# Attention and soft mixture of experts on one core: the second expert layer cut into units of 128, 256 and 128 columns

## The chip, the cores and the metric

The kernel runs on one core of a Trainium2 chip. The metric is the device time of one execution in microseconds (us). Everything is fp32.

## The reference

Two steps follow each other. The first is an attention between 512 tokens `x` and 32 states in each of 8 batches and 8 heads; its output, tokens and states together, is a matrix `x` of 8 * 544 rows and 512 columns. The second is a soft mixture of 8 experts with 4 slots each:

```python
logits = x @ phi                                  # 4352 x 32
d = softmax over the rows (axis 0) of logits
slot_input = d.T @ x                              # 32 slots x 512
for e in range(8):
    h = np.maximum(slot_input[e] @ w1[e], 0.0)    # 4 x 1024
    slot_out[e] = h @ w2[e]                       # 4 x 512
c = softmax over the slots (axis 1) of logits
return c @ slot_out                               # 4352 x 512
```

The weights `w1` (8 x 512 x 1024) and `w2` (8 x 1024 x 512) are 16 MB each, so a core must read some 32 MB of weights and 8 MB of `x` and write some 9 MB of output.

## The kernel before, in words

The program has three stages. The attention is written as a table of steps (`ORDER`, lines 30 to 56) that is walked at line 679; it ends with the 32 slot inputs. Then comes the first expert layer: `w1_part` (line 695) adds up `h_ps` for the two halves `hf` of the 1024 hidden columns, `h_copy` brings a half to SBUF, `h_turn` (line 714) transposes it, and `h_relu` (line 719) sums and clips it into `h_m[hf]`. Then comes the second layer with the output.

The change is in the last stage. The 512 columns of `w2` are handled in **units**: a unit has a PSUM tile `so[k]` in which the products of all 8 experts and both hidden halves are added up (16 parts of 4 matmuls of 32 rows, `part` at line 756). Before, unit 0 has columns 0 to 255, unit 2 columns 256 to 383 and unit 3 columns 384 to 511. When a unit is complete,

- `so_copy` (line 774) copies it to SBUF (ACT takes the first 128 columns, DVE the next 128),
- `so_sum` (line 782) adds its four row groups by a matmul with `rep`, for 128 columns at a time, and ACT copies the result into `so_r`,
- `out(k, q)` (line 790) multiplies block `k` of 128 output columns with the token weights of four batches `q` (4 matmuls of 512 columns), ACT and DVE copy two of the four results each into a tile `out`, and SyncE (SP) stores it by one DMA of 1024 KB; `out(0, 0)` alone is stored in two halves. `out_st` does the same for the states, `out_by_batches` for block (3, 0), in two halves.

The order of PE's work is written out by hand at lines 874 to 914: between the `out` blocks stand calls `more(n)`, which issue the next `n` parts of the units that are still to come. Every DMA of weights and of outputs is issued by SP, in the order of the program, so that all go through one queue. `load_w` (line 108) issues the weights from the list `todo`, one at a time, whenever a buffer of the attention has become free; `load_part` (line 136) puts three experts of `w2` into small buffers (`st_phi`, four `h` tiles, `sv`). The last weights, two tiles `w2b` of 2048 KB, are issued during the first layer at line 707.

Of the kernel before, what the change touches and what calls it, by code (L numbers as in the profile page):

```python
# [8 lines left out]
F32 = mybir.dt.float32  # L9
# [6 lines left out]
P = 128  # L16
B = 8
S = 512
NS = 32
D = 64  # L20
E = 8
F = 1024
# [34 lines left out]
SR_BUFS = 1  # L57
AN = 2

GROUPS = ((0, 1), (2, 3), (4, 5), (6, 7))  # L60


@with_exitstack
def attention_soft_moe(ctx: ExitStack, tc: tile.TileContext, x0, x1, x, st0, st1, w1, w2a, w2b, out_x, out_s):

# [3 lines left out]
    nc = tc.nc  # L71
    pe, act, dve, pool = nc.tensor, nc.scalar, nc.vector, nc.gpsimd
# [4 lines left out]
    pairs = ctx.enter_context(tc.tile_pool(name="pairs", bufs=NPAIR))  # L77


    st_phi = cp.tile([P, F + 4 * NS], F32, name="st_phi")  # L80
# [3 lines left out]
    for b in range(B):  # L84
        t = big.tile([P, 4, NJ, 2 * D], F32, tag="big", name=f"x{b}")
# [14 lines left out]

    w1t, w2t = {}, {}
    todo = [(1, hf, e) for hf in range(2) for e in range(E)]
    todo += [(2, k, e) for k in range(2) for e in range(0, E, 2)]
    last = todo.pop()
    todo += [(3, 0, 0), (3, 0, 4), last, (3, 1, 0), (3, 1, 4)]
    both = []

    def load_w(n):
        for _ in range(min(n, len(todo))):
            layer, k, e = todo.pop(0)  # L110
            if layer == 3:
                t = pairs.tile([P, 4 * F], F32, tag="pair", name=f"w3_{k}_{e}")
                t = t.rearrange("p (e k f) -> p e k f", e=4, k=8)
                nc.sync.dma_start(t, w2b[e // 4, k])
                for i in range(32):
                    w2t[3, k, e + i // 8, i % 8] = t[:, i // 8, i % 8]
                continue
            if layer == 1 and len(w1t) < 8 * NPAIR:
                if not both:
                    t = pairs.tile([P, 4 * F], F32, tag="pair", name=f"w1_{k}_{e}")  # L120
                    both.extend((t[:, 0 : 2 * F], t[:, 2 * F :]))
                t = both.pop(0)
            else:
                t = big.tile([P, 2 * F], F32, tag="big", name=f"w{layer}_{k}_{e}")
            if layer == 1:
                t = t.rearrange("p (k f) -> p k f", k=4)
                nc.sync.dma_start(t, w1[k, e])
                for i in range(4):
                    w1t[k, e, i] = t[:, i]
            else:  # L130
                t = t.rearrange("p (e k f) -> p e k f", e=2, k=4)
                nc.sync.dma_start(t, w2a[e // 2, k])
                for i in range(8):
                    w2t[layer, k, e + i // 4, i % 4] = t[:, i // 4, i % 4]

    def load_part(t, k, e, ft):
        n = t.shape[1] // 256
        t = t.rearrange("p (k f) -> p k f", k=n)
        nc.sync.dma_start(t, w2a[e // 2, k][:, e % 2, ft : ft + n])
        for i in range(n):  # L140
            w2t[2, k, e, ft + i] = t[:, i]

    def st_t(b, g):
        return stT_sb[:, b // 2, g % 2, g // 2, b % 2, :]
# [29 lines left out]
    with ExitStack() as actx:  # L174
        wk = actx.enter_context(tc.tile_pool(name="work", bufs=1))
# [14 lines left out]
        def half(name):  # L190
            return wk.tile([P, S], F32, tag="h", name=name, bufs=NH)
# [483 lines left out]

        states_read = max(order.index(f"S.{B - 1}"), order.index("U.1"))
        halves_had = max(order.index(t) for t in order if t.split(".")[0] in ("q", "aT", "e2", "ee", "ed", "windows"))
        (k1, e1), (k2, e2) = [todo.pop(B)[1:] for _ in range(2)]
        for i, step in enumerate(order):
            name, *args = step.split(".")  # L680
            steps[name](*map(int, args))
            if i == states_read:
                load_part(st_phi[:, 0:F], k1, e1, 0)
            if i == halves_had:
                for k, e in ((k1, e1 + 1), (k2, e2)):
                    for ft in (0, 2):
                        load_part(half(f"w2_{k}_{e}_{ft}"), k, e, ft)
        load_part(wk.tile([P, 2 * S], F32, tag="sv", name=f"w2_{k2}_{e2 + 1}", bufs=1), k2, e2 + 1, 0)


        h_ps = [ps_s.tile([P, 512], F32, tag="sc", name=f"h_ps{i}") for i in range(2)]
# [22 lines left out]
        def h_turn(hf):  # L714
            hT[hf] = ps_t.tile([P, 4, P], F32, tag="tr", name=f"hT_ps{hf}")
            for ft in range(4):
                pe.transpose(hT[hf][:, ft, :], h_sb[hf][:, P * ft : P * ft + P], ident)

        def h_relu(hf):
            t = sm.tile([P, 4, NS], F32, tag="tt", name=f"hT{hf}", bufs=1)  # L720
            dve.tensor_reduce(out=t, in_=hT[hf].rearrange("p f (k n) -> p f n k", k=4), axis=AX.X, op=ALU.add)
            for ft in range(4):
                dve.tensor_scalar_max(slots(h_m[hf], ft), t[:, ft, :].rearrange("p (e c) -> p e c", c=4), 0.0)
# [28 lines left out]


        so, so_sb, so_r = {}, {}, {}

        def part(k, hf, e, cols, w):
            if hf == 0 and e == 0:
                so[k] = ps_s.tile([P, cols], F32, tag="sc", name=f"so_ps{k}")
            for i in range(4):
                pe.matmul(  # L760
                    so[k][32 * i : 32 * i + 32, :],
                    h_m[hf][:, 256 * i + 32 * e : 256 * i + 32 * e + 32],
                    w(i),
                    start=(hf == 0 and e == 0),
                    stop=(hf == 1 and e == E - 1),
                )

        def wide_part(hf, e):
            part(0, hf, e, 256, lambda i: w2t[2, hf, e, i])

        def w2_part(k, hf, e):
            part(k, hf, e, P, lambda i: w2t[3, k - 2, e, 4 * hf + i])

        def so_copy(k):
            cols = so[k].shape[1]
            so_sb[k] = half(f"so_sb{k}")[:, 0:cols]
            act.copy(so_sb[k][:, 0:P], so[k][:, 0:P])
            if cols > P:
                dve.tensor_copy(so_sb[k][:, P:cols], so[k][:, P:cols])

        def so_sum(k, half_of=0):
            c = slice(P * half_of, P * half_of + P)
            p = mtile([P, P], f"sum_ps{k}_{half_of}")
            pe.matmul(p, rep, so_sb[k][:, c], start=True, stop=True)
            i = k + half_of
            if i % 2 == 0:
                so_r[i // 2] = half(f"so_r{i // 2}")[:, 0:256]
            act.copy(so_r[i // 2][:, P * (i % 2) : P * (i % 2) + P], p)

        def out(k, q):  # L790
            hf, col = k // 2, 128 * (k % 2)
            o = [(ps_t if j % 2 else ps_m).tile([P, 512], F32, tag="tr" if j % 2 else "ms", name=f"o{k}_{q}_{j}")
                 for j in range(NJ)]
            for j in range(NJ):
                rows = slice(32 * j, 32 * j + 32)
                pe.matmul(  # L796
                    o[j],
                    so_r[hf][rows, col : col + 128],
                    lt_all[rows, 4 * q : 4 * q + 4, :].rearrange("p b s -> p (b s)"),
                    start=True,  # L800
                    stop=True,
                )
            ot = big.tile([P, NJ, 512], F32, tag="big", name=f"out{k}_{q}")
            to = out_x[k, q].rearrange("p j s -> (p j s)").rearrange("(i p j s) -> i p j s", i=2, p=P, j=2)
            for jp in range(2):
                act.copy(ot[:, 2 * jp, :], o[2 * jp])  # L806
                dve.tensor_copy(ot[:, 2 * jp + 1, :], o[2 * jp + 1])  # L807
                if (k, q) == (0, 0):
                    nc.sync.dma_start(to[jp], ot[:, 2 * jp : 2 * jp + 2, :])
            if (k, q) != (0, 0):  # L810
                nc.sync.dma_start(out_x[k, q], ot)

        def out_by_batches(k, q):
            hf, col = k // 2, 128 * (k % 2)
# [56 lines left out]
                        c_back(i)  # L871
            h_copy(hf)

        for e in range(E):
            wide_part(0, e)
            if e == 3:
                h_turn(1)
                h_relu(1)
        for e in range(E):
            wide_part(1, e)  # L880

        rest = [(k, hf, e) for k in (2, 3) for hf in range(2) for e in range(E)]

        def more(n):
            for _ in range(n):
                w2_part(*rest.pop(0))

        so_copy(0)
        more(1)
        so_sum(0)  # L890
        more(1)
        so_sum(0, 1)
        out(0, 0)
        more(5)
        out(0, 1)
        more(5)
        out(1, 0)
        more(4)
        so_copy(2)
        out(1, 1)  # L900
        so_sum(2)
        more(4)
        out_st(0)
        out_st(1)
        out(2, 0)
        more(6)
        out(2, 1)
        more(6)
        so_copy(3)
        out_st(2)  # L910
        so_sum(3)
        out_by_batches(3, 0)
        out_st(3)
        out(3, 1)
# [35 lines left out]
```

## Time and profile before

| what | value |
|---|---|
| median of 3 runs | 129.48 us (129.45 to 129.86) |
| the profiled execution | 129.54 us, of which its span is 127.8 us |
| PE busy | 116.7 us, 91% of the span |
| DVE, ACT, POOL busy | 68%, 60%, 35% |
| DMA | 51.74 MB, mean 405 GB/s |
| DMA busy share | full (9 of 9) in all of the 40 slices but the first and the last |

A busy share of the DMA is the mean over 16 DMA engines. "To landing" is the time from the start of a DMA's issue on SP until the last of its engines has reported its part. The chain of waits is the work that ended last, followed back from the end; a line of it gives the start, the length and the work.

### The profile page before, as it was taken

The page shows a single profiled execution, that of the slowest core. Times are in us where ns is not written, and L with a number is a line of the kernel's source. Part 1 is how long each engine was busy: PE and PEld are TensorE (multiplying, and loading weights), DVE is VectorE, ACT ScalarE, POOL GpSimd, SP SyncE. Part 2 cuts the span into 40 slices and gives each one's busy share as a digit, 9 for nine tenths or more (in the row PEclk, how much of TensorE's full clock was granted, in tenths as well). Part 3 has the DMA queues.
Part 4 walks back from the last instruction along what each step waited for, and adds up shares of the span by engine and source line. Part 5 has one row for each costly group of instructions (what it writes and reads, how often), then busy time and mean ns, then how long its engine had stood idle before and what let it go on. Part 6 is the DMA issues. An engine that isn't in the chain of part 4 may idle for free.

```text
span 127.8 us, 4698 instructions
## 1 busy us (share of the span) xinstructions
PE 116.7 (91%) x1992; PEld 80.5 (63%) x1992; DVE 86.7 (68%) x194; ACT 76.9 (60%) x189; POOL 44.8 (35%) x63
## 2 busy tenths in 40 slices
PE   5989999999999999999999999999999999998600
PEld 2737686789686869858767869952465655575200
DVE  2348999999999999999986759019930355442700
ACT  4039999999999999999965711310100445635700
POOL 3005266391947467557882105803500000000000
PEclk9999999999999999999999999999999999999955
DMA  4999999999999999999999999999999999999993
GB/s 130 345 410 423 423 426 423 428 423 421 423 423 426 416 436 416 421 431 418 426 418 433 416 421 398 448 423 441 413 441 415 436 383 412 421 419 420 386 430 139
DMA packets 8229, 51.74 MB, mean 405 GB/s; under 512 B 912, under 2 KB 1040, under 8 KB 3216
## 3 DMA queue, kind: packets, MB, share of 16 engines
q1 hardware_dynamic: 7920, 50.92, 95.9%
q10 hardware_dynamic: 288, 0.52, 1.1%
q8 instruction: 15, 0.25, 0.7%
q14 instruction: 6, 0.05, 0.1%
HBM read 42.53 MB, written 8.91 MB: 403 GB/s over the span
## 4 chain that ended last, share of the span: by engine, by line
PE 72%; DVE 10%; DMA 6%; ACT 3%; issue 2%; SPq 1%; POOL 0%; DVEq 0%; ACTq 0%; POOLq 0%
PE so_ps L760 12%; PE h_ps L697 11%; PE xt_ps L226 8%; PE o L796 7%; DMA st_phi<-st_in 6%; PE sc L245 5%; PE sr_ps L343 4%; PE an_ps L309 4%; PE eT_ps L309 4%; PE lt L378 3%; PE t_ps L503 2%; DVE sums L274 2%; DVE q L258 2%; DVE aT L290 1%; DVE m L263 1%
## 5 line engine op out<-in xcount | busy, mean ns | idle before, releaser
L267 POOL TENSOR_TENSOR q<-q,m 128x512 f32<-128x512 f32 x16 | 16.8, 1051 | 15.7 <-DVE m L263 5.2
L231 ACT ACTIVATE xt<-xt_ps 128x512 f32<-128x512 f32 x30 | 18.0, 618 | 5.7 <-PE xt_ps L226 5.5
L226 PE MATMUL xt_ps<-ident,x 128*128 128x128 f32 x128 | 18.4, 282 | 0.5 <-DMA x<-x_in 0.5
L285 POOL TENSOR_TENSOR q<-q,rr 128x512 f32<-128x512 f32 x16 | 16.6, 1051 | 5.1 <-DVE rr L280 3.6
L226 PEld LDWEIGHTS xt_ps<-ident,x 128*128 128x128 f32 x128 | 14.6, 144 | 3.8 <-PE sc L245 1.4
L760 PE MATMUL so_ps<-w,h_m 128*32 128x128 f32 (+1 forms) x376 | 15.5, 309 | 0.0
L807 DVE COPY out<-o 128x512 f32<-128x512 f32 x14 | 9.2, 687 | 9.0 <-PE o L796 8.8
L760 PEld LDWEIGHTS so_ps<-w,h_m 128*32 128x32 f32 x376 | 10.4, 110 | 7.2 <-issue 4.6
L697 PE MATMUL h_ps<-w,si_m 128*32 128x512 f32 x128 | 14.4, 594 | 0.1
L296 DVE TENSOR_REDUCE nm<-sc 128x1 f32<-128x512 f32 x16 | 10.6, 670 | 2.2 <-PE sc L245 2.2
L806 ACT COPY out<-o 128x512 f32<-128x512 f32 x14 | 7.7, 588 | 6.8 <-PE o L796 6.7
L697 PEld LDWEIGHTS h_ps<-w,si_m 128*32 128x32 f32 x128 | 9.1, 110 | 3.9 <-issue 2.9
L301 ACT ACTIVATE e<-sc,nm 128x512 f32<-128x512 f32 x16 | 11.3, 709 | 0.4 <-DVE nm L296 0.2
L258 DVE STREAM_TRANSPOSE q<-sc 128x512 f32<-128x512 f32 x16 | 11.1, 695 | 0.1
L290 DVE STREAM_TRANSPOSE aT<-q 128x512 f32<-128x512 f32 x16 | 10.9, 689 | 0.3 <-POOL q L285 0.2
L343 PE MATMUL sr_ps<-x,eT 128*32 128x64 f32 x512 | 10.5, 221 | 0.1
L274 DVE TENSOR_REDUCE sums<-q 128x16 f32<-128x512 f32 x16 | 10.4, 663 | 0.2 <-ACT q L270 0.2
L263 DVE TENSOR_REDUCE m<-q 128x16 f32<-128x512 f32 x16 | 10.4, 658 | 0.0
L270 ACT ACTIVATE q<-q 128x512 f32<-128x512 f32 x16 | 10.4, 650 | 0.0
L309 PE MATMUL eT_ps<-ident,e 128*128 128x128 f32 x64 | 9.8, 279 | 0.0
L245 PE MATMUL sc<-xt,st_phi 64*32 64x512 f32 x128 | 9.6, 601 | 0.0
L343 PEld LDWEIGHTS sr_ps<-x,eT 128*32 128x32 f32 x512 | 8.7, 110 | 1.5 <-issue 1.0
(126 smaller groups left out, 186.2 us busy)
## 6 DMA issues: line engine op xcount, KB each, us to landing
w<-w_in SPq DMA_DIRECT2D x16, 1024.0 KB, 19.7
w<-w2b_in SPq DMA_DIRECT2D x4, 2048.0 KB, 15.0
x<-x_in SPq DMA_DIRECT2D x7, 1024.0 KB, 13.9
w<-w2a_in SPq DMA_DIRECT2D x6, 1024.0 KB, 19.5
out_x<-out SPq DMA_DIRECT2D x6, 1024.0 KB, 5.8
out_x<-out SPq DMA_DIRECT2D x4, 512.0 KB, 4.7
w<-w2a_in SPq DMA_DIRECT2D x4, 256.0 KB, 14.5
x<-x_in ACTq DMA_DIRECT2D x2, 256.0 KB, 3.9
```

Source lines behind the costliest of these rows:

```text
L226: pe.transpose(p[:, P * j : P * j + P], xb[b][:, g, j, :], ident)
L231: act.mul(r[f"xt{g}"], r[f"xp{g}"], 0.125)
L245: pe.matmul(r[f"sp{h}"][32 * g : 32 * g + 32, :], st_t(b, g)[64 * h : 64 * h + 64, :], r[f"xt{g}"][64 * h : 64 * h + 64, :], start=True, s ...
L258: dve.transpose(r[f"q{h}"], r[f"sp{h}"])
L267: pool.tensor_tensor(v, v, R[b][f"m1{h}"].broadcast_to([P, 16, NS]), op=ALU.subtract)
L274: dve.tensor_reduce(out=v, in_=R[b][f"qv{h}"], axis=AX.X, op=ALU.add)
L285: pool.tensor_tensor(v, v, r.broadcast_to([P, 16, NS]), op=ALU.mult)
L290: dve.transpose(r[f"aT{h}"], r[f"q{h}"])
L309: pe.transpose(p[:, j, :], r[f"{src}{h}"][:, P * j : P * j + P], ident)
L343: pe.matmul(r["srp"][32 * g : 32 * g + 32, h, :], r[f"eT{h}"][:, j, 32 * g : 32 * g + 32], xb[b][:, g, j, D * h : D * h + D], start=(j == ...
L697: pe.matmul(h_ps[hf][32 * kt : 32 * kt + 32, :], si_m[kt // 2][:, 256 * (kt % 2) + 32 * e : 256 * (kt % 2) + 32 * e + 32], w1t[hf, e, kt], ...
L760: pe.matmul(so[k][32 * i : 32 * i + 32, :], h_m[hf][:, 256 * i + 32 * e : 256 * i + 32 * e + 32], w(i), start=(hf == 0 and e == 0), stop=( ...
```

## The change

The units become 128, 256 and 128 columns wide: unit 0 is columns 0 to 127, unit 1 is 128 to 383, unit 2 is 384 to 511. One function `more(u, n)` issues the next `n` parts of unit `u`. Unit 2 takes experts 0 to 3 of both hidden halves before experts 4 to 7. The weights are laid out anew in HBM to match (`w2q`, `w2h`, `w2g`, `w2r`), with as many DMAs of the same sizes in the same places of SP's queue. The order of PE's work is written anew, and `out(0, 0)` is stored by one DMA.

```diff
+UNITS = ((0, 128), (128, 256), (384, 128))
...
-    todo += [(2, k, e) for k in range(2) for e in range(0, E, 2)]
-    last = todo.pop()
-    todo += [(3, 0, 0), (3, 0, 4), last, (3, 1, 0), (3, 1, 4)]
+    todo += [(2, 0, e) for e in range(0, E, 2)]
+    todo += [(3, 0, 4), (4, 0, 0), (4, 0, 4), (3, 0, 6), (5, 0, 0), (5, 0, 4)]
...
-        def wide_part(hf, e):
-            part(0, hf, e, 256, lambda i: w2t[2, hf, e, i])
-
-        def w2_part(k, hf, e):
-            part(k, hf, e, P, lambda i: w2t[3, k - 2, e, 4 * hf + i])
+        rest = [[(hf, e) for hf in range(2) for e in range(E)] for _ in UNITS]
+        rest[2].sort(key=lambda t: t[1] // 4)
+
+        def more(u, n):
+            for _ in range(n):
+                hf, e = rest[u].pop(0)
+                first, last = u not in so, not rest[u]
+                if first:
+                    so[u] = ps_s.tile([P, UNITS[u][1]], F32, tag="sc", name=f"so_ps{u}")
+                for i in range(4):
+                    pe.matmul(
+                        so[u][32 * i : 32 * i + 32, :],
+                        h_m[hf][:, 256 * i + 32 * e : 256 * i + 32 * e + 32],
+                        w2t[u, e, 4 * hf + i],
+                        start=first,
+                        stop=last,
+                    )
...
             for jp in range(2):
                 act.copy(ot[:, 2 * jp, :], o[2 * jp])
                 dve.tensor_copy(ot[:, 2 * jp + 1, :], o[2 * jp + 1])
-                if (k, q) == (0, 0):
-                    nc.sync.dma_start(to[jp], ot[:, 2 * jp : 2 * jp + 2, :])
-            if (k, q) != (0, 0):
-                nc.sync.dma_start(out_x[k, q], ot)
+            nc.sync.dma_start(out_x[k, q], ot)
...
-        for e in range(E):
-            wide_part(0, e)
-            if e == 3:
-                h_turn(1)
-                h_relu(1)
-        for e in range(E):
-            wide_part(1, e)
...
+        more(0, 6)
+        h_turn(1)
+        h_relu(1)
+        more(0, 2)
+        more(1, 2)
+        more(0, 8)
         so_copy(0)
-        more(1)
+        more(1, 1)
         so_sum(0)
-        more(1)
-        so_sum(0, 1)
+        more(1, 1)
         out(0, 0)
-        more(5)
+        more(1, 4)
         out(0, 1)
-        more(5)
+        more(1, 8)
+        so_copy(1)
+        more(2, 2)
+        so_sum(1)
+        more(2, 1)
+        so_sum(1, 1)
         out(1, 0)
-        more(4)
-        so_copy(2)
+        more(2, 4)
         out(1, 1)
-        so_sum(2)
-        more(4)
+        more(2, 4)
         out_st(0)
         out_st(1)
         out(2, 0)
-        more(6)
+        more(2, 5)
+        so_copy(2)
         out(2, 1)
-        more(6)
-        so_copy(3)
+        so_sum(2)
         out_st(2)
-        so_sum(3)
         out_by_batches(3, 0)
```

How this moves PE's instructions is seen at two places. The first is the end of unit 0 up to the first output block (`so_ps` is a unit's PSUM tile, `h_m` the hidden values, `o_0_0` the first product of a block; `x4` is four matmuls). Before, PE has:

```order
L760 MATMUL so_ps_1784<-w_1_5_1654,h_m_1659 32x256 x4
L760 MATMUL so_ps_1784<-w_1_6_1722,h_m_1659 32x256 x8
L760 MATMUL so_ps_1863<-w_0_0_1685,h_m_1658 32x128 x4
L784 MATMUL sum_ps_0_1868<-so_sb_1860,rep 128x128
L760 MATMUL so_ps_1863<-w_0_0_1685,h_m_1658 32x128 x4
L784 MATMUL sum_ps_1_1876<-so_sb_1860,rep 128x128
L796 MATMUL o_0_0_1879<-lt_all,so_r_1870 128x512
```

and with the change:

```order
L767 MATMUL so_ps_1784<-w_0_4_1122,h_m_1659 32x128 x8
L767 MATMUL so_ps_1784<-w_0_6_1278,h_m_1659 32x128 x8
L767 MATMUL so_ps_1828<-w_2_0_1520,h_m_1658 32x256 x2
L767 MATMUL so_ps_1828<-w_2_2_1522,h_m_1658 32x256 x2
L785 MATMUL sum_ps_0_1875<-so_sb_1869,rep 128x128
L767 MATMUL so_ps_1828<-w_3_1654,h_m_1658 32x256 x4
L797 MATMUL o_0_0_1883<-lt_all,so_r_1877 128x512
```

Unit 0 ends in narrow matmuls, one sum instead of two stands ahead of the first block, and the filling comes from the wide unit 1. The second place is PE between the last product of block (0, 1) and the first of block (1, 0). Before:

```order
L796 MATMUL o_1_3_1917<-lt_all,so_r_1870 128x512
L760 MATMUL so_ps_1863<-w_0_4_1695,h_m_1658 32x128 x4
L760 MATMUL so_ps_1863<-w_0_0_1685,h_m_1659 32x128 x16
L796 MATMUL o_0_0_1948<-lt_all,so_r_1870 128x512
L796 MATMUL o_0_1_1949<-lt_all,so_r_1870 128x512
```

With the change:

```order
L797 MATMUL o_1_3_1916<-lt_all,so_r_1877 128x512
L767 MATMUL so_ps_1828<-w_0_1685,h_m_1659 32x256 x16
L767 MATMUL so_ps_1828<-w_4_1695,h_m_1659 32x256 x16
L767 MATMUL so_ps_1962<-w_0_1724,h_m_1658 32x128 x8
L785 MATMUL sum_ps_0_1971<-so_sb_1959,rep 128x128
L767 MATMUL so_ps_1962<-w_0_1724,h_m_1658 32x128 x4
L785 MATMUL sum_ps_1_1978<-so_sb_1959,rep 128x128
L797 MATMUL o_0_0_1982<-lt_all,so_r_1877 128x512
```

Where 20 narrow matmuls stood between the two blocks, there are now 32 wide ones, 12 narrow ones and both sums of unit 1.

## Rows read from the trace of the kernel before

**Rows 1.** The page's line on what the core read and wrote.
```profile
HBM read 42.53 MB, written 8.91 MB: 403 GB/s over the span
```
**Rows 2.** Stretches: length, PE, PEld, DVE, ACT, POOL busy; clock, DMA share, GB/s.
```profile
20.00:40.00 20.00, 19.87 (x417) 15.64 (x407) 19.61 (x41) 19.57 (x47) 11.02 (x13) 1.00 1.01 423
102.00:106.00 4.00, 4.00 (x84) 2.09 (x76) 1.99 (x4) 1.55 (x4) 0.00 (x0) 1.00 0.92 383
119.00:121.00 2.00, 1.42 (x8) 0.30 (x4) 1.44 (x3) 1.44 (x3) 0.00 (x0) 1.00 0.89 367
102.17:127.00 24.83, 17.88 (x292) 10.01 (x284) 9.87 (x17) 10.42 (x25) 0.00 (x0) 0.88 0.93 387
```
**Rows 3.** Timeline of SP, 84 to 122 us: start, length, issue of a DMA.
```profile
84.63 0.90 SPq L114 DMA_DIRECT2D w<-w2b_in  x2
102.17 0.94 SPq L809 DMA_DIRECT2D out_x<-out  x2
105.07 0.33 SPq L811 DMA_DIRECT2D out_x<-out  x1
107.37 0.33 SPq L811 DMA_DIRECT2D out_x<-out  x1
109.45 0.33 SPq L811 DMA_DIRECT2D out_x<-out  x1
121.24 0.35 SPq L811 DMA_DIRECT2D out_x<-out  x1
```
**Rows 4.** Time to landing of issues at 85.1, 102.2, 102.8, 105.1, 107.4, 109.5 us.
```profile
w<-w2b_in SPq DMA_DIRECT2D x1, 2048.0 KB, 20.7
out_x<-out SPq DMA_DIRECT2D x1, 512.0 KB, 5.0
out_x<-out SPq DMA_DIRECT2D x1, 512.0 KB, 5.6
out_x<-out SPq DMA_DIRECT2D x1, 1024.0 KB, 5.7
out_x<-out SPq DMA_DIRECT2D x1, 1024.0 KB, 5.9
out_x<-out SPq DMA_DIRECT2D x1, 1024.0 KB, 6.3
```
**Rows 5.** Time to landing of the last issue, at 121.24 us.
```profile
out_x<-out SPq DMA_DIRECT2D x1, 1024.0 KB, 5.6
```
**Rows 6.** Chain of waits, 90.9 to 103.7 us: start, length, work.
```profile
90.95 1.73 PE so_ps L760 x32
92.68 0.59 PE hT_ps L717 x4
93.26 5.36 PE so_ps L760 x96
...
99.02 0.49 PE sum_ps L784 x2
...
99.87 0.42 PE sum_ps L784 x2
...
101.35 1.23 PE so_ps L760 x40
102.58 1.07 PE o L796 x8
```
**Rows 7.** Timeline of DVE, 94 to 106 us: start, length, work.
```profile
94.03 0.44 DVE L723 TENSOR_SCALAR h_m<-hT 128x32 f32<-128x32 f32 x4
...
103.72 1.29 DVE L807 COPY out<-o 128x512 f32<-128x512 f32 x2 [1.01 <-PE o L796]
```
**Rows 8.** First DMA issue on SP at the start of the program (timeline).
```profile
0.74 0.86 SPq L89 DMA_DIRECT2D x<-x_in  x2
```
**Rows 9.** Stretches as in rows 2, around the first bytes moved.
```profile
1.60:1.70 0.10, 0.10 (x1) 0.10 (x2) 0.10 (x1) 0.05 (x1) 0.10 (x1) 1.00 0.00 0
1.80:1.90 0.10, 0.10 (x1) 0.06 (x1) 0.10 (x2) 0.10 (x1) 0.00 (x0) 1.00 1.87 143
```
**Rows 10.** DMA queues, whole span: packets, MB, share of 16 engines' span.
```profile
q8 instruction: 15, 0.25, 0.7%
```
**Rows 11.** The same queue from 112 to 114 us.
```profile
q8 instruction: 1, 0.02, 2.7%
```

More of the change, by code (lines that the diff above doesn't have):

```diff
@@ L58, with attention_soft_moe @@
 AN = 2
+UNITS = ((0, 128), (128, 256), (384, 128))
 GROUPS = ((0, 1), (2, 3), (4, 5), (6, 7))
 @with_exitstack
-def attention_soft_moe(ctx: ExitStack, tc: tile.TileContext, x0, x1, x, st0, st1, w1, w2a, w2b, out_x, out_s):
+def attention_soft_moe(ctx: ExitStack, tc: tile.TileContext, x0, x1, x, st0, st1, w1, w2q, w2h, w2g, w2r, out_x, out_s):
     nc = tc.nc
@@ L110, in load_w @@
             layer, k, e = todo.pop(0)
[L111 to L116, printed above, removed]
+            if layer in (4, 5):
+                t = pairs.tile([P, 4 * F], F32, tag="pair", name=f"w{layer}_{e}")
+                n = 4 if layer == 4 else 8
+                t = t.rearrange("p (e k f) -> p e k f", e=4, k=n)
+                nc.sync.dma_start(t, (w2g if layer == 4 else w2r)[e // 4])
+                for i in range(4 * n):
+                    u, ft = (1, 4) if layer == 4 else (2, 0)
+                    w2t[u, e + i // n, ft + i % n] = t[:, i // n, i % n]
                 continue
@@ L130, in load_w, with load_part @@
             else:
[L131 to L136, printed above, removed]
+                n = 8 if layer == 2 else 4
+                t = t.rearrange("p (e k f) -> p e k f", e=2, k=n)
+                nc.sync.dma_start(t, (w2q if layer == 2 else w2h)[e // 2])
+                for i in range(2 * n):
+                    w2t[layer - 2, e + i // n, i % n] = t[:, i // n, i % n]
+    def load_part(t, e, ft):
         n = t.shape[1] // 256
         t = t.rearrange("p (k f) -> p k f", k=n)
-        nc.sync.dma_start(t, w2a[e // 2, k][:, e % 2, ft : ft + n])
+        nc.sync.dma_start(t, w2h[e // 2][:, e % 2, ft : ft + n])
         for i in range(n):
-            w2t[2, k, e, ft + i] = t[:, i]
+            w2t[1, e, ft + i] = t[:, i]
     def st_t(b, g):
@@ L677, in attention_soft_moe @@
         halves_had = max(order.index(t) for t in order if t.split(".")[0] in ("q", "aT", "e2", "ee", "ed", "windows"))
-        (k1, e1), (k2, e2) = [todo.pop(B)[1:] for _ in range(2)]
         for i, step in enumerate(order):
@@ L682, in attention_soft_moe @@
             if i == states_read:
-                load_part(st_phi[:, 0:F], k1, e1, 0)
+                load_part(st_phi[:, 0:F], 0, 0)
             if i == halves_had:
-                for k, e in ((k1, e1 + 1), (k2, e2)):
+                for e in (1, 2):
                     for ft in (0, 2):
-                        load_part(half(f"w2_{k}_{e}_{ft}"), k, e, ft)
-        load_part(wk.tile([P, 2 * S], F32, tag="sv", name=f"w2_{k2}_{e2 + 1}", bufs=1), k2, e2 + 1, 0)
+                        load_part(half(f"w2_{e}_{ft}"), e, ft)
+        load_part(wk.tile([P, 2 * S], F32, tag="sv", name="w2_3", bufs=1), 3, 0)
         h_ps = [ps_s.tile([P, 512], F32, tag="sc", name=f"h_ps{i}") for i in range(2)]
@@ L754, in attention_soft_moe @@
         so, so_sb, so_r = {}, {}, {}
[L756 to L766, printed above, removed]
-        def wide_part(hf, e):
-            part(0, hf, e, 256, lambda i: w2t[2, hf, e, i])
-        def w2_part(k, hf, e):
-            part(k, hf, e, P, lambda i: w2t[3, k - 2, e, 4 * hf + i])
+        rest = [[(hf, e) for hf in range(2) for e in range(E)] for _ in UNITS]
[14 more added lines that the diff above has]
+                    )
         def so_copy(k):
@@ L784, in so_sum @@
             pe.matmul(p, rep, so_sb[k][:, c], start=True, stop=True)
-            i = k + half_of
+            i = UNITS[k][0] // P + half_of
             if i % 2 == 0:
@@ L803, in out @@
             ot = big.tile([P, NJ, 512], F32, tag="big", name=f"out{k}_{q}")
-            to = out_x[k, q].rearrange("p j s -> (p j s)").rearrange("(i p j s) -> i p j s", i=2, p=P, j=2)
             for jp in range(2):
@@ L872, in attention_soft_moe @@
             h_copy(hf)
-        for e in range(E):
-            wide_part(0, e)
-            if e == 3:
-                h_turn(1)
-                h_relu(1)
-        for e in range(E):
-            wide_part(1, e)
[L882 to L886, printed above, removed]
+        more(0, 6)
[4 more added lines that the diff above has]
+        more(0, 8)
         so_copy(0)
-        more(1)
+        more(1, 1)
         so_sum(0)
-        more(1)
-        so_sum(0, 1)
+        more(1, 1)
         out(0, 0)
-        more(5)
+        more(1, 4)
         out(0, 1)
-        more(5)
+        more(1, 8)
[4 more added lines that the diff above has]
+        so_sum(1, 1)
         out(1, 0)
-        more(4)
-        so_copy(2)
+        more(2, 4)
         out(1, 1)
-        so_sum(2)
-        more(4)
+        more(2, 4)
         out_st(0)
@@ L933 @@
         "w1_in": con(moe_w1.reshape(E, 4, P, 2, 512).transpose(3, 0, 2, 1, 4)),
-        "w2a_in": con(moe_w2[:, :, :256].reshape(E // 2, 2, 2, 4, P, 256).transpose(0, 2, 4, 1, 3, 5)),
-        "w2b_in": con(moe_w2[:, :, 256:].reshape(E // 4, 4, 8, P, 2, P).transpose(0, 4, 3, 1, 2, 5)),
+        "w2q_in": con(moe_w2[:, :, :128].reshape(E // 2, 2, 8, P, P).transpose(0, 3, 1, 2, 4)),
+        "w2h_in": con(moe_w2[:, : F // 2, 128:384].reshape(E // 2, 2, 4, P, 256).transpose(0, 3, 1, 2, 4)),
+        "w2g_in": con(moe_w2[:, F // 2 :, 128:384].reshape(E // 4, 4, 4, P, 256).transpose(0, 3, 1, 2, 4)),
+        "w2r_in": con(moe_w2[:, :, 384:].reshape(E // 4, 4, 8, P, P).transpose(0, 3, 1, 2, 4)),
     }
@@ L944 @@
     ox = r["out_x"].copy()
-    ox[0, 0] = ox[0, 0].reshape(2, P, 2, 512).transpose(1, 0, 2, 3).reshape(P, 4, 512)
     ox[3, 0] = ox[3, 0].reshape(2, P, 4, 256).transpose(1, 2, 0, 3).reshape(P, 4, 512)
```

## The prediction, made before the changed kernel was run

> **What bounds the kernel now.** The page puts PE at 91%, which invites one to count matmuls. I began there, but the change leaves their number and shapes alone: 64 wide and 128 narrow ones of the second layer, four sums, the same output blocks. The question is then what the order does to the end of the run, and the end is a store. So I read the DMA rows before any other. From 20 to 40 us the 16 DMA engines are busy by a share of 1.01 at 423 GB/s [rows 2], which is how "full" reads here; 51 MB at that rate fill most of the span. The stores are 8.91 MB [rows 1], 21 us of that rate.
>
> The issues and their landings make a ladder [rows 3, 4]. The last weights are issued at 85.1 and land 20.7 later, at 105.8. The two halves of the first output land at 102.2 + 5.0 = 107.2 and 102.8 + 5.6 = 108.4, block (0, 1) at 105.07 + 5.7 = 110.8, (1, 0) at 107.37 + 5.9 = 113.3, (1, 1) at 109.45 + 6.3 = 115.8. That is one rung of 2.4 to 2.5 us for each 1024 KB, and the last store, issued at 121.24, lands at 126.8 [rows 3, 5]: 16.0 us after block (0, 1) for the remaining 6.5 MB, again 2.46 for each. A landing is reported by the DMA engine that is last. So the last engine never waited for SP, from the weights to the end. The mean engine did wait a little: its share was 0.92 from 102 to 106 and 0.89 from 119 to 121 [rows 2], against 1.01. That is 4 x 0.09 + 2 x 0.12 = 0.6 us lost by engines that are ahead of the last one.
>
> The reader should see two things. Making PE faster gains nothing while stores are issued ahead of the last engine; and the queue must never run empty, since a pause of all engines adds to the end in full.
>
> **The change, part by part.** *Weights.* SP issues the same number of DMAs of the same sizes and, by the shapes in the code, the same run of bytes in each partition, in the same places. Each tile is needed later than it lands: the latest, the second `w2r`, has the place of the DMA that landed at 105.8, and its first matmul comes after block (1, 1), later than 109 by the account below. Cost 0.
>
> *First output stored whole.* The two halves took 108.4 - 105.8 = 2.6 us of ladder, a whole block 2.4 [rows 3, 4]; rounding is 0.1 in each. I take a gain of 0.1, with ends 0 and 0.2.
>
> *PE's order.* I take prices from the chain [rows 6]. A matmul shows as two instructions there; 20 narrow matmuls took 1.23, 0.0615 each. The stretch of 5.36 holds 48 wide and 4 narrow ones by PE's order, so a wide one takes (5.36 - 0.25) / 48 = 0.1065. A block takes 1.07, a sum 0.43 to 0.49, the transposes 0.59. From the end of a unit to the start of its sum is 99.02 - (93.26 + 5.36 - 0.25) = 0.65 at least, which is ACT's copy and its handshakes. PE starts the second layer at 90.95. With the change:
>
> - 24 narrow (1.48), transposes (0.59), 8 narrow (0.49), 8 wide (0.85): 94.36. DVE's part for the other half ended at 94.03 + 0.44 = 94.47, or 1.2 after the transposes [rows 6, 7], here about 94.2: just covered.
> - 32 narrow (1.97): unit 0 complete at 96.33. Its sum starts at 96.98 after 0.65, since the 4 wide ones between are shorter; the sum and 4 wide ones with a switch take 0.95: block (0, 0) runs from 97.95 to 99.02. Before, it began after the sum that starts at 99.87.
> - From the end of a block on PE to the issue of its store: block (0, 1) ended at 102.58 + 1.07 = 103.65, DVE's second copy at 103.72 + 1.29 = 105.01, the issue came at 105.07 [rows 3, 6, 7], 1.42 later. So the first store is issued at **100.4**, and whole, instead of in halves from 102.17.
> - 16 wide (1.70), block (0, 1): ends at 101.8, store at **103.2** instead of 105.07.
> - 32 wide (3.41): unit 1 complete at 105.2; 0.65; a sum, 4 narrow, a sum (1.2 together): block (1, 0) runs from 107.0 to 108.1, store at **109.5** instead of 107.37.
>
> So the first two stores come 1.8 us earlier, and the third comes 2.1 us later. Between the second and the third SP issues nothing for 6.3 us, where the longest such pause was 2.3.
>
> *What that does to the queue.* From 102.17 to the end 24.83 us at 387 GB/s were moved [rows 2], 9.61 MB, of which 8.91 are stores: 0.70 MB of weights were left at 102.17. At 100.4 it is 0.70 + 1.73 x 0.423 = 1.43 MB, with the first store 2.48. At 103.2 it is 2.48 - 1.17 + 1.05 = 2.36 MB, which last 5.6 us: the mean engine is empty at **108.8**. The next store is issued at 109.5. How soon its bytes move is seen on empty engines at the start: SP begins the first issue at 0.74, nothing moves before 1.7, and the share is full by 1.9 [rows 8, 9], so 1.0. The mean engine is therefore empty from 108.8 to 110.5, **1.7 us**. The losses of 0.6 us that it had before go, as the queue is deep at both places. Net 1.1 us for the mean engine.
>
> The first-byte latency given by the Trainium skill for this path (DMA: Bandwidth & Descriptors, section Specifications) is about 0.6 us. The row at the start says 1.0, and the row decides; by the page's figure the sum would be 0.4 us lower, at 130.0.
>
> *What it does to the end.* The last engine lands block (0, 1) at 110.8 - 0.1 = 110.7 and needs the next store just then; if issued at 109.5 plus 1.0, its bytes begin at 110.5, so this engine waits hardly at all. But now all engines start level, and the slack of those that were ahead is gone. What used that slack? PE's instructions arrive through the same engines: 15 packets, 0.7% of 16 x 127.8 us together [rows 10], 0.95 us each, on one engine at a time. One falls between 112 and 114 (2.7% of 32 us, 0.86) [rows 11]; the rungs around it kept their 2.45, so it fell on an engine that was ahead. With the change about as many PE instructions remain behind that point, so it comes near 113 again, after the pause, on an engine that has nothing in hand any more. That engine ends 0.9 later. The two accounts agree: 1.1 for the mean engine, 0 for the last one as it was, +0.9 for the one that becomes last.
>
> Nothing behind it can give this back: the rest of PE's order has the same work, its last store was issued 5.6 us before landing and may come up to 2 us later or earlier without being felt.
>
> Sum: 129.54 (the profiled execution, 127.8 of span and 1.74 around it; 0.06 above the median of 129.48) + 0.9 = 130.4.
>
> **The rivals.**
>
> 1. *The same work moves at the same rate, no change.* The bytes are the same and the ladder was unbroken. If block (1, 0) is issued at 109.0 or earlier, or if the instruction packet falls on an engine that is still ahead, the last engine's ladder stays as it is: 129.54 - 0.1 = 129.4. This speaks for it: my time for the issue carries four waits of 0.1 to 0.3, and without any of them it is 108.9. Against it: half of 6.3 us of pause would already equal the deepest rest in the queue before. The Trainium skill gives a ceiling of 435 GB/s (same page and section), by which nothing but the number of bytes counts; the 423 of the row are near it, and the pause is what that rule leaves out.
>
> 2. *The third store comes later still.* If PE's sums wait for ACT, or the second unit for its copies, by 0.6 more, the last engine starves too and every tenth is felt: issue at 110.1, 131.0 us. For it: two of the four sums now follow directly on each other, where before one was always hidden behind a block. Against it: no such stall above 0.4 is in the chain before.
>
> 3. *Faster.* The early first stores fill the 0.36 us that the mean engine loses between 102 and 106, and the third is in time. It would have to be issued before about 108.5, less than the sum of PE's pure work allows (108.9), and the last engine's ladder would also have to shrink, which has no gap: at best the 0.1 of the whole store and some tenths, 129.1.
>
> **How the numbers follow.** A measurement of this kernel can tell about 0.3%, 0.39 us, from no change. The forecast, a pause that sets the engines level and moves the end by 0.5 to 1.3 us, has 0.63, its own range 129.9 to 130.8. Rival 1 has 0.22, rival 2 0.10, rival 3 0.05. Slower by over 0.3% is 0.73, within it 0.22, faster 0.05. The range for 8 in 10 takes in rivals 1 and 2 up to their centres: 129.3 to 131.1.
>
> **What would show it.** Right: SP issues the stores near 100.4, 103.2 and 109.5; the DMA share falls to some 0.6 between 107 and 111 and is full from 111 on to near the end; the landings of (0, 1) and (1, 0) lie 2.5 to 2.9 us apart, and the later rungs stretch by the instruction packet; PE's last matmul ends no later than before (121), with the span some 0.9 us longer. Wrong: a share near 1.0 through 107 to 111 (PE was quicker than I think, and nothing changes), or a dip there with the last landing still at 126.8 (the engines that paused had more in hand than I think), or a PE that waits for weights.

## The result, and the profile after

The changed kernel is **slower by 1.0%**: 130.96 us (median of 8 runs) against 129.57 us for the kernel before beside it (8 runs), ratio 1.0097, 95% interval 1.0068 to 1.0127. Measured a second time, beside the experiments, it was 130.60 against 129.74 us, ratio 1.0068 (1.0053 to 1.0082). Forecast were 130.4 us and 0.9 us of loss; the losses measured are 1.39 and 0.86 us. Both times lie in the range for 8 in 10 (129.3 to 131.1), the first 0.16 us above the narrower range of the mechanism (129.9 to 130.8).

The profiled execution took 130.67 us, 1.13 more than the one before, all of it in the span (127.8 to 128.9). The page has the same bytes and the same PE share; the DMA line is no longer full:

```profile
span 128.9 us, 4695 instructions
PE 117.5 (91%) x1992; PEld 81.2 (63%) x1992; DVE 86.8 (67%) x194; ACT 76.8 (60%) x189; POOL 44.8 (35%) x63
DMA  3999999999999999999999999999999996899992
HBM read 42.53 MB, written 8.91 MB: 399 GB/s over the span
```

Each digit of the DMA line is 3.2 us; the 6 and the 8 cover 106 to 113 us. Stretches of the changed kernel (length; PE, PEld, DVE, ACT, POOL busy; clock, DMA share, GB/s) show where:

```profile
102.00:106.00 4.00, 4.00 (x82) 2.50 (x74) 1.39 (x3) 1.13 (x3) 0.00 (x0) 1.00 0.99 414
107.00:111.00 4.00, 4.00 (x81) 2.19 (x80) 2.06 (x4) 2.16 (x5) 0.00 (x0) 1.00 0.66 268
111.00:119.00 8.00, 7.76 (x94) 4.27 (x86) 4.41 (x9) 5.22 (x15) 0.00 (x0) 1.00 1.01 420
119.00:121.00 2.00, 1.38 (x8) 0.30 (x4) 1.44 (x3) 1.43 (x3) 0.00 (x0) 1.00 0.99 416
```

The two dips of before, 0.92 and 0.89 [rows 2], are filled (0.99 and 0.99). In their place stands one deeper: 0.66 over the four microseconds from 107 to 111, in which PE is busy throughout. Against a full 1.01 that is 1.4 us of the mean engine, for 0.5 gained at the old dips (4 x 0.07 + 2 x 0.10): 0.9 net.

SP's issues (start, length) and the time to landing of each of the four, in the same order:

```profile
100.25 0.35 SPq L808 DMA_DIRECT2D out_x<-out  x1
103.19 0.34 SPq L808 DMA_DIRECT2D out_x<-out  x1
109.50 0.33 SPq L808 DMA_DIRECT2D out_x<-out  x1
111.58 0.33 SPq L808 DMA_DIRECT2D out_x<-out  x1
```
```profile
out_x<-out SPq DMA_DIRECT2D x1, 1024.0 KB, 8.4
out_x<-out SPq DMA_DIRECT2D x1, 1024.0 KB, 7.9
out_x<-out SPq DMA_DIRECT2D x1, 1024.0 KB, 4.7
out_x<-out SPq DMA_DIRECT2D x1, 1024.0 KB, 5.1
```

The last engine's ladder is 108.7, 111.1, **114.2**, 116.7: one rung of 3.1 where all were 2.4 to 2.5 before [rows 3, 4]. The store that took 5.7 to 6.3 us to land behind others takes 4.7 here, since it finds the queue nearly empty, and yet it lands 0.9 later than before (113.3). The last store, issued at 121.44, lands 6.6 later:

```profile
121.44 1.14 SPq L808 DMA_DIRECT2D out_x<-out  x1
```
```profile
out_x<-out SPq DMA_DIRECT2D x1, 1024.0 KB, 6.6
```

That is 128.0 against 126.8 [rows 3, 5]: 0.9 was lost by the third store, 0.3 more on the 13.8 us behind it (13.5 before). PE's end did not decide it: its last store was issued at 121.44 against 121.24 and waited longer in the queue.

A landing is the last of 16 reports, one from each DMA engine, and the trace holds them all. For the third store, block (1, 0), and the last, block (3, 1), in us:

| reports | first | median | 15th | 16th |
|---|---|---|---|---|
| third store, before | 111.16 | 111.88 | 113.21 | 113.25 |
| third store, with the change | 113.15 | 113.23 | 113.49 | 114.23 |
| last store, before | 125.44 | 126.22 | 126.77 | 126.83 |
| last store, with the change | 126.75 | 126.82 | 127.76 | 128.06 |

The pause sets the engines level: with the change fifteen of them report the third store within 0.34 us, where before they were spread over 2.1. One comes 0.74 behind the fifteenth, and at the end two are about 1 us behind the others. The mean of the 16 is 0.85 later at the last store (126.97 against 126.12), the 16th 1.23.

Why the third store is late stands in the chain of waits of the changed kernel (start, length, work):

```profile
96.71 0.49 PE sum_ps L785 x2
...
97.77 1.07 PE o L797 x8
98.84 1.86 PE so_ps L767 x32
100.70 1.07 PE o L797 x8
101.77 4.03 PE so_ps L767 x80
105.80 0.44 PE sum_ps L785 x2
106.24 0.35 PE so_ps L767 x8
106.59 0.42 PE sum_ps L785 x2
107.01 1.07 PE o L797 x8
```

Between the blocks (0, 1) and (1, 0) PE works 4.03 us on the units and 1.2 on two sums, where 1.23 stood before [rows 6].

### The profile page after: what moved, and what is told of

The parts are those of the page before. It is cut to its first block, busy times and chain, and to the rows that moved or that the text cites. A ratio compares the mean times of both kernels' runs of the same rounds, so it can differ in the third digit from the quotient of the medians.

```text
span 128.9 us, 4695 instructions
## 1 busy us (share of the span) xinstructions
PE 117.5 (91%) x1992; PEld 81.2 (63%) x1992; DVE 86.8 (67%) x194; ACT 76.8 (60%) x189; POOL 44.8 (35%) x63
## 4 chain that ended last, share of the span: by engine, by line
PE 70%; DVE 14%; DMA 6%; issue 1%; SPq 1%; POOL 0%; ACT 0%; DVEq 0%; POOLq 0%
PE so_ps L767 12%; PE h_ps L699 11%; PE xt_ps L229 8%; PE o L797 7%; DMA st_phi<-st_in 6%; PE sc L248 5%; PE an_ps L312 4%; PE eT_ps L312 4%; PE sr_ps L346 4%; PE lt L381 2%; DVE sums L277 2%; DVE q L261 2%; PE t_ps L506 2%; DVE aT L293 2%; DVE nm L299 2%
```

## The experiments

Two rivals of the queue were to be excluded (the new layout of the weights; PE as the bound), and its rule had to be made exact: is it the length of the pause, or whether the bytes issued so far last until the next store? All ratios are to the kernel before, run beside each. The change run again stood beside three of them: the second store later (again), the first store in halves, and the narrow units with the third store at 108.

| kernel | third store issued at (profile) | ratio (95% interval) |
|---|---|---|
| the change | 109.50 | 1.0097 (1.0068 to 1.0127) |
| the change again | 109.42 | 1.0068 (1.0053 to 1.0082) |
| second store later | 109.26; again 109.60 | 1.0052 (1.0027 to 1.0077); again 1.0066 (1.0039 to 1.0092) |
| third store 2 us later | 111.24 | 1.0169 (1.0141 to 1.0198) |
| the kernel before, third store late | 109.03 | 1.0081 (1.0053 to 1.0109) |
| first store in halves | 109.13 | 1.0050 (1.0036 to 1.0064) |
| four narrow units | 106.97; again 106.58 | 1.0004 (0.9984 to 1.0024); again 0.9994 (0.9978 to 1.0011) |
| narrow units, third at 108 | 108.27 | 1.0061 (1.0040 to 1.0082) |
| narrow units, third at 108, no stall | 107.65 | 1.0063 (1.0040 to 1.0086) |
| narrow units, late tail | 106.50 | 1.0082 (1.0055 to 1.0108) |

### The second store later, the third unmoved

```diff
         out(0, 0)
-        more(1, 4)
-        out(0, 1)
         more(1, 8)
+        out(0, 1)
+        more(1, 4)
```

> The changed kernel, but block (0, 1) is computed after eight instead of four parts of unit 1, so that its store goes out about 1.7 us later (104.9 instead of 103.2) and the third where it was (109.5). The pause between two issues shrinks from 6.3 to 4.6 us. Queue theory (what counts is whether the bytes issued by then last until the third store): the same bytes are issued before 108.8, the queue is empty at the same time, nothing changes: ratio to the kernel before 1.010 as for the change, 1.007 to 1.013. Rival, the length of the pause counts: it shrinks by 1.7 us, ratio 1.000 or below.

1.0052, outside both expectations, nearer to the queue's. So it was run again beside the changed kernel:

> The kernel with the second store 1.5 us later and the third where it was, once more, now beside the changed kernel itself. Queue theory: the two are equal within 0.3 us, since the same bytes are issued by the third store. Rival (the length of the pause counts): it is 0.4 us or more faster than the changed kernel.

> The changed kernel once more, as a measure for the others on the same chip: ratio to the kernel before 1.007 to 1.013, as measured first.

1.0066 and 1.0068: equal. The pause between two issues is 4.6 us instead of 6.3, and it makes no difference. The length of a pause is not what counts.

### The kernel before, with its third store late

```diff
         out(0, 1)
-        more(5)
+        more(9)
+        so_copy(2)
+        more(4)
         out(1, 0)
-        more(4)
-        so_copy(2)
-        out(1, 1)
         so_sum(2)
-        more(4)
+        out(1, 1)
```

> The kernel before, with its units and layout, but eight parts (2 us of PE) that stood behind block (1, 0) now stand ahead of it, so that its store goes out near 109.5 instead of 107.4; the first two stores stay at 102.2 and 105.1. Queue theory: by 109.5 the same bytes have been issued as with the change, so the queue runs empty as there: ratio 1.006 to 1.012, with a DMA share well under 1 around 109. Rival, layout or unit widths cost and not the late store: ratio 0.998 to 1.002.

1.0081: with the old units and the old layout, the late third store costs as much as the change (the fourth goes out 1.4 us later with it). Its profile shows something more. Issues of blocks (0, 1), (1, 0) and (1, 1), their landings in that order, and PE's instruction queue from 112 to 114 us:

```profile
104.99 0.33 SPq L811 DMA_DIRECT2D out_x<-out  x1
109.03 0.33 SPq L811 DMA_DIRECT2D out_x<-out  x1
110.83 0.33 SPq L811 DMA_DIRECT2D out_x<-out  x1
```
```profile
out_x<-out SPq DMA_DIRECT2D x1, 1024.0 KB, 5.9
out_x<-out SPq DMA_DIRECT2D x1, 1024.0 KB, 4.3
out_x<-out SPq DMA_DIRECT2D x1, 1024.0 KB, 6.2
```
```profile
q8 instruction: 1, 0.02, 3.3%
```

The landings are 110.9, 113.3 and 117.0. The third store's rung is 2.4: the last engine did not wait for it at all. The next rung is 3.7, in the stretch in which a packet of PE's instructions comes in (3.3% of 32 us, 1.06 us). Before, a packet in the same stretch took 0.86 us and stretched no rung [rows 4, 11]. The reports say the same: fifteen engines land block (1, 1) between 115.14 and 115.76, one at 117.04. The trace does not name the engine of a packet; but the packet of instructions ends at 113.74, and the one data packet that starts with its end (113.73) takes 0.70 us, where its neighbours take 0.31. That this engine is the late one is read from these rows; no run was made to move the packet.

### Four narrow units

```diff
-UNITS = ((0, 128), (128, 256), (384, 128))
+UNITS = ((0, 128), (128, 128), (256, 128), (384, 128))
...
-            w2t[1, e, ft + i] = t[:, i]
+            w2t[1, e, ft + i] = t[:, i, 0:P]
+            w2t[2, e, ft + i] = t[:, i, P:]
...
         out(0, 1)
-        more(1, 8)
+        more(1, 4)
         so_copy(1)
-        more(2, 2)
+        more(2, 3)
         so_sum(1)
-        more(2, 1)
-        so_sum(1, 1)
+        more(2, 2)
         out(1, 0)
...
```

> The changed kernel with its new weight layout and whole first store, but unit 1 is cut into two units of 128 columns, so that block (1, 0) needs only the first of them; its store should go out near 106.7 instead of 109.5. 64 wide matmuls become 128 narrow ones, about 1.1 us more of PE. Queue theory: no engine runs empty, the last engine's ladder is unbroken again, ratio to the kernel before 0.997 to 1.001 although PE has more to do. Rival, the new layout of the weights costs: ratio stays 1.008 to 1.012. Rival, PE bounds the end: 1.1 us more on top of the change, ratio 1.018.

1.0004, and again:

> The kernel with four narrow units once more, as a measure beside it: ratio to the kernel before 0.998 to 1.003.

0.9994. The whole loss of the change is gone, with its layout, its whole first store and its early first two stores kept, and with 64 wide matmuls made into 128 narrow ones. So layout and units cost nothing that intervals of 0.2% can show, and more PE work costs nothing while the queue is fed. Stretches of the second run (as above), and its third issue:

```profile
102.00:106.00 4.00, 4.00 (x101) 2.64 (x90) 1.56 (x4) 1.86 (x6) 0.00 (x0) 1.00 0.97 406
107.00:111.00 4.00, 4.00 (x86) 2.75 (x86) 1.29 (x2) 2.16 (x6) 0.00 (x0) 1.00 1.00 414
119.00:121.00 2.00, 1.79 (x10) 0.44 (x8) 1.44 (x4) 1.44 (x5) 0.00 (x0) 1.00 0.80 330
```
```profile
106.58 0.33 SPq L819 DMA_DIRECT2D out_x<-out  x1
```

It does not beat the kernel before, though its first stores are 2 us earlier and its share from 102 to 106 is 0.97 instead of 0.92. Its mean engine still runs short later (0.80 from 119 to 121, and as much from 113 to 114), against what I expected; but the time is set by the engine that lands last, and that one was full in both.

### The third store 2 us later still

```diff
         so_sum(1, 1)
+        more(2, 8)
         out(1, 0)
-        more(2, 4)
         out(1, 1)
-        more(2, 4)
```

> The changed kernel, but eight narrow parts of unit 2 (2.0 us of PE) move from behind block (1, 0) to ahead of it: its store goes out near 111.5. Queue theory with level engines: every further tenth of delay is felt by all 16 engines, so the end moves by 2.0 us more, ratio 1.010 + 0.0155 = 1.025, 1.021 to 1.028. If engines still had work in hand (the cost of the change is not the empty queue), less than half of it, ratio under 1.018.

1.0169, above the change but under my 1.021, and inside what I had set for engines that still have work in hand (under 1.018). That bound took 2.0 us of delay and 1.010 for the change. The store moved by 1.74 us (111.24 against 109.50), and its profiled execution, the longest of its six, is 1.63 us longer (132.30 against 130.67), 0.94 for each microsecond of delay. By medians it is 1.2 to 1.5 us, 0.7 to 0.9 for each. The queue is empty in the stretch from 110 to 112, by then also for the last engine:

```profile
107.00:110.00 3.00, 3.00 (x74) 2.19 (x68) 0.11 (x1) 0.33 (x2) 0.00 (x0) 1.00 0.68 281
110.00:112.00 2.00, 2.00 (x12) 1.03 (x8) 1.98 (x4) 1.77 (x4) 0.00 (x0) 1.00 0.08 33
```

The 16 reports decide between the two expectations. All engines land the third store between 114.90 and 115.11, so none had work in hand. The median report of the last store comes at 128.57, 1.75 us after that of the change, for a delay of 1.74. The 16th, at 129.65, comes only 1.59 later, and the reason is the packet of instructions. Here it ran from 108.88 to 109.82, over before the store's bytes came, and no engine lands that store late. With the change it ran from 109.14 to 110.43, and the data packet that starts 0.05 us behind it took 1.18 us, where its neighbours took 0.31. The packet is not all of the end, though: here one engine still lands the last store 1.08 us behind the median. What delays that engine no run shows.

### The first store in halves again

The changed kernel with the two `dma_start` calls of before in `out(0, 0)`.

> The changed kernel with its first output stored in two halves again, as before. My term was 0.1 us (0 to 0.2) for the whole store: this kernel is 0 to 0.2 us slower than the changed kernel beside it. Queue theory: the halves go out at most 0.6 us earlier in part, with the same bytes by the third store, so nothing else changes.

130.32 against 130.60 us, 0.3 us *faster* where I expected up to 0.2 slower. Its profiled third store went out at 109.13, 0.29 before the one beside it, and the stores behind the halves are the same. This difference is as large as that between two profiled executions of one kernel (109.26 and 109.60 with the second store later). What it shows is that the whole store gains nothing.

### Narrow units with the third store near 108

```diff
-        more(2, 2)
+        more(2, 6)
         out(1, 0)
-        more(2, 4)
         out(1, 1)
```

> The kernel with four narrow units, but four narrow parts (1.0 us) move ahead of block (1, 0), so that its store goes out near 108.0 instead of 107.0. Queue theory: the mean engine is empty at 108.8 and bytes move 0.8 to 1.0 after an issue, so only engines that are ahead wait: no change against the kernel before, ratio 0.998 to 1.003. Rival, any delay of the third store costs its own length: ratio 1.008.

1.0061: the expectation failed, and the rival's 1.008 lies inside the interval. But PE stalled between the two blocks that now follow each other, and its profile has a second pause: block (3, 0) goes out at 120.1 instead of 119.4, and the DMA share from 119 to 121 is 0.67 instead of 0.74. To separate the two, the next kernel left four of the parts between the blocks:

> Four narrow units, four narrow parts moved ahead of block (1, 0) as in the kernel with the third store near 108, but four parts stay between blocks (1, 0) and (1, 1), so that PE does not stall there and the stores from (2, 0) on go out as with the four narrow units alone ((3, 0) near 119.4 instead of 120.1). If that kernel's 0.6% came from its late tail (a second pause of the mean engine after 119): ratio to the kernel before 0.999 to 1.003. If it came from the third store at 108: ratio 1.004 to 1.008 again.

1.0063, in the range that I had set for the third store as the cause. But in its profile (3, 0) still went out late, at 119.8, with a share of 0.72 (119.0 and 0.80 in the second run of the four narrow units). And the last engine lands block (2, 1) at 121.25, no later than there (121.33): up to that point the later third store had cost this engine nothing. So the tail alone was made late, with the third store where it had cost nothing:

```diff
         out(2, 1)
+        warm(384)
         more(3, 9)
```

> The kernel with four narrow units, third store left near 107, with one idle matmul of 384 columns (about 0.75 us of PE, its result unused) behind block (2, 1), so that only the last stores, (3, 0) and (3, 1), go out later: (3, 0) near 120.0 as in the two kernels with the third store near 108. If the 0.6% of those two came from their late tail: ratio to the kernel before 1.003 to 1.007. If it came from the third store at 108: ratio 0.998 to 1.002.

1.0082 with the third store at 106.50, above the 1.003 to 1.007 that I had set for the tail. The late tail by itself costs as much as both of them. Its profile (the quickest of its six executions), from 107 to 109 and from 119 to 121 us, with the issue of block (3, 0):

```profile
107.00:109.00 2.00, 2.00 (x62) 1.70 (x60) 1.29 (x2) 1.17 (x3) 0.00 (x0) 1.00 1.00 418
...
119.00:121.00 2.00, 1.99 (x18) 0.87 (x10) 1.56 (x5) 1.67 (x6) 0.00 (x0) 1.00 0.60 250
```
```profile
119.78 0.33 SPq L842 DMA_DIRECT2D out_x<-out  x1
```

The idle matmul took 0.84 us of PE, block (3, 0) went out 0.76 later than in the second run of the four narrow units (119.02), and the median is 0.9 to 1.0 us longer (130.68 against 129.78 and 129.69). The profiled execution shows 0.4 to 0.5 of it (130.04 against 129.67 and 129.54); where the rest of the median comes from is not shown. The engines are level again here: all 16 land the first half of (3, 0) between 122.20 and 122.77, against 121.45 to 122.58 in the second run of the four narrow units. So the queue has a second place where it can run short, and I had looked at the wrong one. Whether a third store near 108 costs anything by itself stays open: both kernels that tried it also had the late tail, and cost no more than that tail alone.

## Why the prediction was right

*The bound.* That stores are paid only through the queue was right: four narrow units add PE work for nothing, and the late third store costs in the old units too.

*PE's order.* The sum of prices gave stores at 100.4, 103.2 and 109.5; they went out at 100.25, 103.19 and 109.50. The block (1, 0) ran from 107.01, forecast 107.0. The 0.65 us from the end of a unit to its sum, and the 1.42 from block to issue, made these right; the pure sum of matmuls would have given 108.9.

*The queue.* Forecast was a mean engine that is empty for 1.7 us, with a share near 0.6 from 107 to 111; measured 1.4 and 0.66. Of the 0.6 us of the old dips 0.5 was gained. A net loss of 1.1 was forecast, 0.9 came. One reading was wrong: 2.3 us was not the longest pause between stores before, since they went out at 112.53, 115.62 and 118.67, 3.1 apart. Nothing hangs on it, as the length of a pause is not what counts.

*The first byte.* I took 1.0 us from issue to first byte and not the 0.6 that the Trainium skill gives (DMA: Bandwidth & Descriptors, section Specifications). By the page's figure the sum, an estimate, was 130.0, by the row's 130.4; measured were 130.6 to 131.0. On the queue that a pause has emptied, in the run with the third store 2 us later, the trace shows 0.8: issued at 111.24, no byte before 112.0, full from then on.

*The end.* The last engine's rung was to stay and a later packet of PE's instructions to cost 0.9. The amount came, but not quite the way: in the changed kernel the packet came in at the end of the pause, not near 113, and the lengthened rung is that of the third store itself. From 109 to 111 us its instruction queue shows

```profile
q8 instruction: 1, 0.02, 4.0%
```

4.0% of 32 us, 1.28 us. In the old units with the late store the mechanism ran just as forecast: rung kept, packet after it, 3.7 us. The term that was too small is what follows: I let the rungs behind run as before, and they took 0.3 us more, so that the profile shows 1.13 for the 0.9 forecast. The median engine did run as before, 13.6 us from the third store to the last (113.23 to 126.82); the 16th report took 13.8. That the sum came so near is partly luck. At the last store a second engine is 0.94 behind the median (the 15th report, 127.76), so by these reports the run without the packet would have ended only some 0.3 us earlier, an estimate (128.06 - 127.76). Engines set level, each delay of a single one paid in full: that was right. That one packet was the only such delay was not, and what holds up the second engine stays open. So does why the first measurement lost 1.39 us, more than the 1.13 of its profiled execution.

*The whole first store.* Taken as 0.1 of gain. The run with the halves shows none, and the first two rungs of the changed kernel (108.7, 111.1) stand 0.3 later than those of before (108.4, 110.8), not earlier; in the profile of the change run again they stand level with them (108.4, 110.8).

*The rivals.* "No change" fell, though the bytes are the same; the ceiling of 435 GB/s in the Trainium skill (same page and section) bounds a queue that is fed, and from 107 to 111 this one moved 268. "Later still" was made in a run of its own, and every microsecond cost 0.7 to 0.9 by the medians, 0.94 by the profiles. "Faster" had no mechanism, as said: the four narrow units have the early stores without the pause and gain nothing.

*The tail.* That the last stores could come up to 2 us later without being felt was said of the last engine's ladder alone, and the runs contradict it where the tail was tried: with narrow units 0.84 us more of PE there cost 0.9 to 1.0. It did not enter the sum, since the change leaves PE's end where it was (last store 121.44 against 121.24).

## What to carry to other kernels

When the transfers fill the span, the order of the compute is a schedule for the queue: write down when each store is issued and how many bytes lie in front of it, and let no store come later than those bytes last. Bringing a first store forward draws the same bytes earlier and gained nothing by itself here; what must be shortened is the compute ahead of the store at which the bytes run out, even at the price of more compute. And look at the tail too: 0.8 us of PE ahead of the last two blocks cost as much there as some 2 us ahead of the third.

## What the runs showed that was not expected

- A pause that the last DMA engine does not feel still costs. In the old units with the late third store this engine's rung stayed at 2.4 us, and the run was 0.8% longer. Engines that are ahead are a reserve: single packets that fall on one engine (16 KB of PE's instructions, 0.86 to 1.28 us in the rows here) are absorbed by it, and a pause uses it up. That the packets are PE's is read from their number: 15 in the kernels whose page counts 1992 matmul instructions, 16 in those of four narrow units, with 2120 or more.
- With the queue empty, a store of 1024 KB issued at 111.24 landed 3.9 us later. With a rung of 2.45 for the transfer some 1.45 are left for both ends, 0.8 of it ahead of the first byte. Its issue, its time to landing, and two stretches around the first byte:

```profile
111.24 0.33 SPq L808 DMA_DIRECT2D out_x<-out  x1
```
```profile
out_x<-out SPq DMA_DIRECT2D x1, 1024.0 KB, 3.9
```
```profile
111.90:112.00 0.10, 0.10 (x2) 0.00 (x0) 0.10 (x1) 0.10 (x1) 0.00 (x0) 1.00 0.00 0
112.00:112.10 0.10, 0.10 (x1) 0.00 (x0) 0.10 (x1) 0.10 (x1) 0.00 (x0) 1.00 1.15 492
```
